# Moving the one-hot transfers to another queue and reordering the opening of a routed-attention + SwiGLU kernel

## The chip, the core and the metric

One core of a Trainium2 chip runs the whole program. The time is device microseconds of one execution, and the kernel before was executed three times. Five engines run their own instruction streams in order: TensorE (PE, matrix products), VectorE (DVE), ScalarE (ACT), GpSimd (POOL) and SyncE (SP, which here only issues transfers). Transfers (DMAs) can be issued from SP, ACT or POOL, each of which issues its own in program order.

## The reference

Attention over 4 batches x 8 heads x 768 tokens x 64, in which a query may only see keys that were assigned to the same one of 16 clusters, followed by a token-wise feed-forward layer on 3072 tokens x 512:

```python
q_assign = np.argmax(np.einsum('bhsd,hcd->bhsc', q_n, c_n), axis=-1)
k_assign = np.argmax(np.einsum('bhsd,hcd->bhsc', k_n, c_n), axis=-1)
mask = q_assign[:, :, :, None] == k_assign[:, :, None, :]
scores = np.where(mask, scale * np.matmul(q, k.transpose(0, 1, 3, 2)), -1e9)
attn = softmax(scores);  x = np.matmul(attn, v)          # heads side by side: 3072 x 512
xn = x / np.sqrt(np.mean(x * x, axis=-1) + 1e-6) * rms_g
out = (silu(xn @ w_gate) * (xn @ w_val)) @ w_out          # 512 -> 1536 -> 512
```

## The kernel before, in words

**The mask as extra rows.** For each head the transposed queries and keys (64 rows, bf16) get 16 more rows that hold the one-hot vector of the token's cluster. One matrix product of 80 rows then gives the score plus a large constant where the clusters agree; the exponential subtracts that constant, so all other pairs vanish. These 80-row operands are the tiles `qext` and `kext`, one per group of four heads, in a ring of four.

**Groups.** Heads are prepared in eight groups of four. For each head PE transposes q and k (`trans`, L192), ACT copies the result out of PSUM (L194) into `qkT`, POOL casts q into `qext` (`qcast`, L198), DVE or ACT casts k into `kext` (`kcast`, L204 and L206), and POOL casts v (`vcast`, L209). `scores_c` multiplies with the centroids (L225), and DVE finds the winner for four heads at once by transpose, maximum, comparison and transpose (L228 to L237), which leaves the one-hot rows in the tile `oh`. `place` then moves them with small transfers into rows 64 to 79 of `qext` and `kext`: per head two for q and two for k, so 16 for a group (L249).

**Units.** The attention runs in eight units (half a batch of queries, all eight heads). For each head there are three score steps (L264, two products into one PSUM tile of the two-tile pool `ps_s`, then an exponential on ACT, L266), and the products with v (`pv`, 18 products of L280 into the single tile `acc`), which are written one head later. After a unit's last head come the root mean square (`rms`: squares on ACT, L299, then a chain of small DVE operations to L312), four transposes (`tx`, L321), the gate and value products (L332) and one unit later the output products (`o`, L355), the copy out of PSUM (`o_sb`, two buffers, L358) and the write to memory (`out_dram`, L360).

**What sets the order.** Each engine's order is the order in which the Python code writes it. In a unit a list `fill` of other work (output products of the unit before last, feed-forward of the last unit, the preparation of a group two units ahead) is spread over the 24 score steps by estimated cost. So at a unit's border the queue of SP holds the group's loads, then that group's 16 one-hot transfers, then the three writes of the output.

**Opening.** Before the first unit the code prepares groups 0 and 1 by hand: eight `warm` products on a constant tile, then group 0 in two pairs of heads (`t0`, `clusters0`, whose two centroid products for q and k share one PSUM tile of `ps_s`), then group 1 by way of the list `first`, then four more `warm` products. Each `warm` product asks for a PSUM tile of its own from a pool with one buffer. The pool of general PSUM tiles, `ps_g`, has three.

Of the kernel before, what the change touches and what calls it, by code (L numbers as in the profile page):

```python
# [9 lines left out]
F32 = mybir.dt.float32  # L10
# [12 lines left out]
def kernel(  # L23
# [12 lines left out]
    nc = tc.nc  # L36
    B, H, S, D = q.shape
# [39 lines left out]
    def load_qk(n, kq=None):  # L77
        if n >= B * H:
            return
        staged[n] = stage.tile([P, 2, ST, D], F32, tag="qk", name="qk")  # L80
        nc.sync.dma_start(out=staged[n][:, 0], in_=src(q, n))
# [18 lines left out]
    nc.vector.memset(warm, 1.0)  # L100

    def busy(n, first=True):
        for i in range(n):
            warm_ps = ps_a.tile([P, 512], F32, tag="acc", name="warm") if first else \
                ps_g.tile([P, 512], F32, tag="gen", name="warm")
            nc.tensor.matmul(warm_ps, lhsT=warm[:, :P], rhs=warm, start=True, stop=True)  # L106

    busy(WARM)

# [86 lines left out]
    def qcast(g, h):  # L196
        for e in range(2):
            nc.gpsimd.tensor_copy(qext[g % 4][:D, h, e * UQ:(e + 1) * UQ], qkT[g, h // 2][e * D:(e + 1) * D, h % 2, 0])  # L198

    def kcast(g, h, early=False):  # L200
        for e in range(2):
            to, of = kext[g % 4][:D, h, e * UQ:(e + 1) * UQ], qkT[g, h // 2][e * D:(e + 1) * D, h % 2, 1]
            if early:
                nc.scalar.activation(to, of, ACT.Copy, scale=1.0 / ZS)  # L204
            else:
                nc.vector.tensor_scalar_mul(to, of, 1.0 / ZS)  # L206

    def vcast(n):
        nc.gpsimd.tensor_copy(vbf[n // HG % 4][:, n % HG, :, :D], stagedv[n])  # L209
# [1 line left out]

    scT = {}

    scps = {}

    def scores_c(g, m, h0=0, h1=HG, early=False):
        if not early:
            ps = ps_g.tile([P, UQ], F32, tag="gen", name="sc")
        else:
            if m == 0:  # L220
                scps[g, h0] = ps_s.tile([P, 2, 512], F32, tag="s", name="sc")
            ps = scps[g, h0][:, m, :UQ]
        r = slice(32 * h0, 32 * h1)
        for h in range(h0, h1):
            nc.tensor.matmul(ps[32 * h:32 * h + 32], lhsT=cblk[:, g * HG % H + h],  # L225
                             rhs=qkT[g, h // 2][:, h % 2, m], start=True, stop=True)
        sct = asg.tile([P, UQ], F32, tag="scT", name="scT", bufs=2)
        nc.vector.transpose(sct[r], ps[r])  # L228
# [8 lines left out]
        nc.vector.transpose(oh[r], ohT[r])  # L237
        ext = (kext if m else qext)[g % 4]
        put.append((g, ext, oh, h0, h1))

    put = []

    def place(q_):

        (g, *_, h0, h1) = put[0]
        for h in range(h0, h1):
            for _, ext, oh, _, _ in put:
                for e in range(2):
                    q_.dma_start(out=ext[D:D + NC, h, e * UQ:(e + 1) * UQ],  # L249
                                 in_=oh[32 * h + e * NC:32 * h + (e + 1) * NC])  # L250
        put.clear()

# [110 lines left out]
    def group_work(g):  # L363
        w = []
        for h in range(HG):
            n = g * HG + h
            w.append((0.25, lambda h=h: trans(g, h, 0)))

            def second(h=h, n=n):
                trans(g, h, 1)  # L370
                qcast(g, h)
                vcast(n)
                if g > 1:
                    kcast(g, h)
                    load_qk(n + NQ)
                    load_v(n + NV)
            w.append((0.25, second))
        w.append((0.7, lambda: scores_c(g, 0)))
        w.append((0.7, lambda: (scores_c(g, 1), place(nc.sync))))
        return w  # L380

    def spread(a, b):
# [30 lines left out]
        for m in range(2):  # L413
            scores_c(0, m, h, h + 2, True)

    first = group_work(1)
# [7 lines left out]
    clusters0(0)  # L424
    t0(2)
    kcast(0, 1, True)
    t0(3)
    kcast(0, 2, True)
    place(nc.gpsimd)
    vcast(0)  # L430
    vcast(1)
    clusters0(2)
    place(nc.sync)
    for _, f in first[:2]:
        f()
    kcast(0, 3, True)
    for _, f in first[2:4]:
        f()
    vcast(2)
    vcast(3)  # L440
    for _, f in first[4:]:
        f()
    for h in range(HG):
        kcast(1, h)
    busy(4)

    def weights():
        for c in range(CC):
# [81 lines left out]
```

## Time and profile before

| | |
|---|---|
| three runs | 397.69, 400.38, 401.13 us (median 400.38) |
| the profiled execution | 400.98 us, of which the span of instructions is 399.1 us |
| PE busy | 357.4 us, 90% of the span |
| ACT busy | 259.5 us, 65% |
| DVE busy | 240.2 us, 60% |
| POOL busy | 60.7 us, 15% |
| granted clock of PE, mean | 0.97 |
| first exponential of unit 0 | 24.30 us after the span's start |
| first exponentials of units 1, 2, 3, 4 | 48.26, 94.45, 143.79, 189.10 us |

How to read it: rows of the timeline give the start in us, the duration, the engine, the line, what is done and how often (x2: two of them, merged), and in brackets how long the engine had stood idle before and what ended that. Rows of the waits give the total, the number and the longest. Rows of a table of windows give the stretch, then for PE, PE's weight load, DVE, ACT and POOL the busy time and the number of instructions, then the granted clock of PE, the share of the transfer engines and the rate.

### The profile page before, as it was taken

The numbers are of one execution on the slowest core, as the hardware profiler recorded it, in microseconds if no ns is written. First come the engines' busy times: TensorE is split into PE (matmuls) and PEld (weight loads), VectorE is DVE, ScalarE is ACT, GpSimd is POOL, SyncE is SP. The second block draws the span as 40 slices with busy tenths as digits, with TensorE's granted clock in tenths as the row PEclk, the third lists the DMA queues.
The fourth block names the chain that finished last, engine by engine and source line by source line (L and its number), as shares of the span: only waits on it lengthen the run. The fifth ranks groups of instructions, "written<-read, shape, count | busy, mean of one in ns | idle before, by whom it ended". The sixth has DMA issues, their size and how long they took to land.

```text
span 399.1 us, 7988 instructions
## 1 busy us (share of the span) xinstructions
PE 357.4 (90%) x3013; PEld 214.4 (54%) x3031; DVE 240.2 (60%) x584; ACT 259.5 (65%) x459; POOL 60.7 (15%) x124
## 2 busy tenths in 40 slices
PE   7778679989779996999979998899979999999896
PEld 3335346564447643665446654566445655664452
DVE  5871156787546775667736675567745646666432
ACT  3768957776638873788548875588746785784230
POOL 2694001441013100320012200121000000000000
PEclk9998969999989999999989999899999999999999
DMA  8719996706232301232022001100020002000102
GB/s 269 220 23 202 207 293 193 214 23 193 72 116 85 119 8 67 87 119 62 15 84 81 2 5 45 51 2 2 14 87 2 1 2 80 2 0 22 60 2 80
DMA packets 24967, 32.03 MB, mean 80 GB/s; under 512 B 4960, under 2 KB 20832, under 8 KB 24928
## 3 DMA queue, kind: packets, MB, share of 16 engines
q1 hardware_dynamic: 21360, 25.91, 20.2%
q0 software_dynamic: 2992, 4.82, 6.7%
q10 hardware_dynamic: 576, 0.79, 0.6%
q8 instruction: 24, 0.39, 0.4%
q14 instruction: 15, 0.12, 0.1%
HBM read 28.35 MB, written 6.29 MB: 87 GB/s over the span
## 4 chain that ended last, share of the span: by engine, by line
PE 59%; SPq 12%; DVE 11%; ACT 9%; DMA 5%; issue 4%; DVEq 0%; ACTq 0%
PE gate L332 15%; PE val L332 14%; SPq L249 11%; PE s L264 10%; PE acc L280 6%; ACT pT L266 5%; PE tq L192 5%; PE o L355 3%; DMA out_dram<-o_sb 3%; PE sc L225 3%; ACT junk L299 2%; PE warm L106 2%; DVE scT L228 2%; DVE oh L237 1%; PE tx L321 1%
## 5 line engine op out<-in xcount | busy, mean ns | idle before, releaser
L266 ACT ACTIVATE pT<-s,off 128x768 bf16<-128x768 f32 x192 | 170.5, 900 | 57.9 <-PE s L264 57.3
L264 PE MATMUL s<-qext,kext 80*128 80x384 bf16 x384 | 96.6, 335 | 5.0 <-ACT pT L266 3.3
L332 PE MATMUL gate<-xnT,wg 128*128 128x384 bf16 x384 | 81.3, 333 | 0.6 <-DVE th L341 0.3
L332 PE MATMUL val<-xnT,wv 128*128 128x384 bf16 x384 | 80.1, 332 | 0.7 <-DVE scT L228 0.7
L341 DVE SCALAR_TENSOR_TENSOR th<-th,gate 128x384 f32<-128x384 f32 x84 | 46.4, 552 | 49.0 <-ACT th L340 48.6
L355 PE MATMUL o<-wo,gvT 128*128 128x512 bf16 x274 | 68.3, 379 | 0.8
L198 POOL CAST qext<-qkT 64x384 bf16<-64x384 f32 x64 | 32.8, 512 | 205.5 <-ACT qkT L194 201.7
L264 PEld LDWEIGHTS <-kext 80*128 80x128 bf16 x384 | 36.8, 100 | 39.3 <-issue 17.6
L280 PE MATMUL acc<-vbf,pT 128*128 128x65 bf16 x1152 | 50.3, 195 | 7.8 <-ACT pT L266 7.1
L280 PEld LDWEIGHTS <-pT 128*128 128x128 bf16 x1152 | 46.3, 99 | 19.2 <-ACT pT L266 9.6
L340 ACT ACTIVATE th<-gate 128x384 f32<-128x384 f32 x84 | 41.0, 488 | 22.9 <-PE gate L332 22.8
L346 DVE SCALAR_TENSOR_TENSOR gvT<-th,val 128x384 bf16<-128x384 f32 x84 | 46.5, 553 | 12.8 <-PE val L332 7.0
L332 PEld LDWEIGHTS <-wg 128*128 128x128 bf16 x384 | 36.8, 99 | 24.2 <-issue 3.5
L332 PEld LDWEIGHTS <-wv 128*128 128x128 bf16 x384 | 36.8, 99 | 23.7 <-issue 2.8
L194 ACT COPY qkT<-tq 128x384 f32<-128x384 f32 x64 | 29.8, 479 | 24.3 <-PE tq L192 23.8
L355 PEld LDWEIGHTS <-gvT 128*128 128x128 bf16 x288 | 26.8, 97 | 27.0
L192 PE MATMUL tq<-ident_f,qk 128*128 128x128 f32 x192 | 32.1, 287 | 1.1 <-ACT qkT L194 0.9
L358 DVE COPY o_sb<-o 128x512 f32<-128x512 f32 x24 | 15.9, 686 | 24.2 <-DMA out_dram<-o_sb 17.5
L192 PEld LDWEIGHTS tq<-ident_f,qk 128*128 128x128 f32 x192 | 24.3, 146 | 8.9 <-ACT qkT L194 1.8
L321 PE MATMUL tx<-ident,xn 128*128 128x128 bf16 x96 | 10.5, 236 | 17.5 <-DVE o_sb L358 16.4
L206 DVE TENSOR_SCALAR kext<-qkT 64x384 bf16<-64x384 f32 x56 | 21.1, 378 | 4.5 <-ACT qkT L194 3.7
L299 ACT ACTIVATE junk<-x 128x384 bf16<-128x384 f32 (+1 forms) x48 | 19.9, 415 | 3.2 <-DVE x L287 2.7
(59 smaller groups left out, 205.6 us busy)
## 6 DMA issues: line engine op xcount, KB each, us to landing
qk<-in_q_dram SPq DMA_DIRECT2D x32, 192.0 KB, 3.4
vs<-in_v_dram SPq DMA_DIRECT2D x32, 192.0 KB, 3.7
out_dram<-o_sb SPq DMA_DIRECT2D x24, 256.0 KB, 2.1
qk<-in_k_dram SPq DMA_DIRECT2D x28, 192.0 KB, 3.7
wg<-in_moe_w_gate_dram POOLq DMA_DIRECT2D x4, 384.0 KB, 9.9
wv<-in_moe_w_val_dram POOLq DMA_DIRECT2D x4, 384.0 KB, 11.3
wo<-in_moe_w_out_dram POOLq DMA_DIRECT2D x3, 512.0 KB, 16.8
qext<-oh SPq DMA_DIRECT2D x60, 12.0 KB, 1.8
```

Source lines behind the costliest of these rows:

```text
L192: nc.tensor.transpose(ps[:, i * P:(i + 1) * P], qk[:, part, 2 * i:2 * i + 2].rearrange("p t d -> p (t d)"), ident_f)
L194: nc.scalar.copy(qkT[g, h // 2][:, h % 2, part], ps)
L198: nc.gpsimd.tensor_copy(qext[g % 4][:D, h, e * UQ:(e + 1) * UQ], qkT[g, h // 2][e * D:(e + 1) * D, h % 2, 0])
L249: q_.dma_start(out=ext[D:D + NC, h, e * UQ:(e + 1) * UQ], in_=oh[32 * h + e * NC:32 * h + (e + 1) * NC])
L264: nc.tensor.matmul(ps[:, j, :UQ], lhsT=kext[g % 4][:KR, hh, kc * P:(kc + 1) * P], rhs=qext[g % 4][:KR, hh, hf * UQ:(hf + 1) * UQ], start=T ...
L266: nc.scalar.activation(pT[u, h][:, 2 * i:2 * i + 2], ps[:, :, :UQ], ACT.Exp, bias=off, scale=scale * ZS)
L280: nc.tensor.matmul(acc[:, h % 2, t], lhsT=pT[u, h][:, kc, t * P:(t + 1) * P], rhs=vbf[g % 4][:, hh, kc % HT * 2 + kc // HT], start=kc == 0 ...
L332: nc.tensor.matmul(ps, lhsT=w[:, c, f * P:(f + 1) * P], rhs=xnT[u][:, c], start=c == 0, stop=c == CC - 1)
L340: nc.scalar.activation(th, ps, ACT.Tanh, scale=0.5)
L341: nc.vector.scalar_tensor_tensor(th, th, 1.0, ps, op0=ALU.add, op1=ALU.mult)
L346: nc.vector.scalar_tensor_tensor(gvT[u][:, f], gates[u], 0.5, ps, op0=ALU.mult, op1=ALU.mult)
L355: nc.tensor.matmul(outs[u], lhsT=gvT[u][:, f, t * P:(t + 1) * P], rhs=wo[:, f], start=f == 0, stop=f == FC - 1)
```

## The change

- `place` takes two queues, one for the q rows and one for the k rows. Groups 0 and 1 issue q's on POOL and k's on SP (before: the first pair of group 0 on POOL, everything else on SP). From group 2 on all 16 are issued on POOL, none on SP.
- In the opening the two centroid products of a pair of heads each get a PSUM tile of their own. ACT's order becomes all eight copies of group 0, then the casts of two heads, four copies of group 1, the other two casts, four copies. v's loads are split: the first four ahead of the first one-hot transfers on SP, the last four behind. The casts of v for group 1 come after its clusters.
- `warm`: five products instead of eight at the start and two instead of four before unit 0, and the products of one call share one PSUM tile.
- In a unit, `pv` of the head before is written after the second score step of a head rather than after the first.

```diff
-    WARM = 8
+    WARM = 5
     def busy(n, first=True):
+        to = ps_a.tile([P, 512], F32, tag="acc", name="warm") if first else \
+            ps_g.tile([P, 512], F32, tag="gen", name="warm")
         for i in range(n):
-            warm_ps = ps_a.tile(...) if first else ps_g.tile(...)
-            nc.tensor.matmul(warm_ps, lhsT=warm[:, :P], rhs=warm, start=True, stop=True)
+            nc.tensor.matmul(to, lhsT=warm[:, :P], rhs=warm, start=True, stop=True)
...
     def scores_c(g, m, h0=0, h1=HG, early=False):
-        if not early:
-            ps = ps_g.tile([P, UQ], F32, tag="gen", name="sc")
-        else:
-            if m == 0:
-                scps[g, h0] = ps_s.tile([P, 2, 512], F32, tag="s", name="sc")
-            ps = scps[g, h0][:, m, :UQ]
+        ps = ps_s.tile([P, UQ], F32, tag="s", name="sc") if early else ps_g.tile([P, UQ], F32, tag="gen", name="sc")
...
-    def place(q_):
+    def place(qq, kq):
         (g, *_, h0, h1) = put[0]
         for h in range(h0, h1):
-            for _, ext, oh, _, _ in put:
+            for (_, ext, oh, _, _), on in zip(put, (qq, kq)):
                 for e in range(2):
-                    q_.dma_start(out=ext[D:D + NC, h, e * UQ:(e + 1) * UQ],
+                    on.dma_start(out=ext[D:D + NC, h, e * UQ:(e + 1) * UQ],
                                  in_=oh[32 * h + e * NC:32 * h + (e + 1) * NC])
...
-        w.append((0.7, lambda: (scores_c(g, 1), place(nc.sync))))
+        w.append((0.7, lambda: (scores_c(g, 1), place(nc.gpsimd, nc.gpsimd if g > 1 else nc.sync))))
...
-    for n in range(H):
+    for n in range(HG):
         load_v(n)
-    nc.sync.dma_start(out=gcol, ...)
-    kcast(0, 0, True)
     clusters0(0)
     t0(2)
-    kcast(0, 1, True)
     t0(3)
-    kcast(0, 2, True)
-    place(nc.gpsimd)
+    place(nc.gpsimd, nc.sync)
+    for n in range(HG, H):
+        load_v(n)
+    nc.sync.dma_start(out=gcol, ...)
+    kcast(0, 0, True)
+    kcast(0, 1, True)
     vcast(0)
     vcast(1)
     clusters0(2)
-    place(nc.sync)
-    (group 1 by its list, kcast(0, 3) and vcast(2), vcast(3) among it, place(nc.sync))
+    (group 1: trans and qcast of heads 0, 1; kcast(0, 2), kcast(0, 3); place(nc.gpsimd, nc.sync);
+     vcast(2), vcast(3); trans and qcast of heads 2, 3; both scores_c; four vcast; place(nc.gpsimd, nc.sync))
     for h in range(HG):
         kcast(1, h)
-    busy(4)
+    busy(2)
...
                 scores(u, h, i)
-                if i == 0 and (u, h) != (0, 0):
+                if i == 1 and (u, h) != (0, 0):
                     pv(u, h - 1) if h else pv(u - 1, H - 1)
```

**SP's queue at the border of units 2 and 3**, here the last two one-hot transfers of a group (`oh`), the three output writes (`o_sb`) and the next loads, before:

```order
L249 DMA qext0_146<-oh_2136 16x384 x2
L249 DMA kext0_150<-oh_2175 16x384 x2
L360 DMA out_0_dram<-o_sb_2272 128x512
L360 DMA out_0_dram<-o_sb_2317 128x512
L360 DMA out_0_dram<-o_sb_2367 128x512
L81 DMA qk_2430<-in_q_dram 128x384
```

and the same place of SP's queue after the change:

```order
L81 DMA qk_2056<-in_q_dram 128x384
L82 DMA qk_2056<-in_k_dram 128x384
L88 DMA vs_2059<-in_v_dram 128x384
L353 DMA out_0_dram<-o_sb_2259 128x512
L353 DMA out_0_dram<-o_sb_2284 128x512
L353 DMA out_0_dram<-o_sb_2333 128x512
```

The 16 one-hot transfers that stood between the group's last load and the first write are gone from SP.

**POOL's queue in unit 1**, where groups 2 and 3 are prepared one after the other, after the change (the last casts of group 2, `qext2` and `vbf2`, its 16 one-hot transfers, of which the last four are shown as two rows, and the first casts of group 3):

```order
L242 DMA qext2_138<-oh_1199 16x384 x2
L242 DMA kext2_142<-oh_1235 16x384 x2
L198 CAST qext3_139<-qkT_1265 64x384 x2
L209 CAST vbf3_147<-vs_783 128x6x64
L198 CAST qext3_139<-qkT_1265 64x384 x2
```

Before the change the casts of group 3 followed the casts of group 2 directly on POOL.

**ACT's order in the opening**, before (L194 copies out of PSUM, L204 casts k, L266 is the first exponential):

```order
L194 COPY qkT<-tq 128x384 x4
L204 ACTIVATE kext_150<-qkT 64x384 x2
L194 COPY qkT<-tq 128x384 x2
L204 ACTIVATE kext_150<-qkT 64x384 x2
L194 COPY qkT<-tq 128x384 x2
```

and after:

```order
L194 COPY qkT<-tq 128x384 x8
L204 ACTIVATE kext_140<-qkT 64x384 x4
L194 COPY qkT<-tq 128x384 x4
L204 ACTIVATE kext_140<-qkT 64x384 x4
L194 COPY qkT<-tq 128x384 x4
L259 ACTIVATE pT<-s,off 128x768 x22
```

The casts moved behind the copies of the second pair of heads; their number is the same.

More of the change, by code (lines that the diff above doesn't have):

```diff
@@ L102, in busy @@
     def busy(n, first=True):
+        to = ps_a.tile([P, 512], F32, tag="acc", name="warm") if first else \
+            ps_g.tile([P, 512], F32, tag="gen", name="warm")
         for i in range(n):
-            warm_ps = ps_a.tile([P, 512], F32, tag="acc", name="warm") if first else \
-                ps_g.tile([P, 512], F32, tag="gen", name="warm")
-            nc.tensor.matmul(warm_ps, lhsT=warm[:, :P], rhs=warm, start=True, stop=True)
+            nc.tensor.matmul(to, lhsT=warm[:, :P], rhs=warm, start=True, stop=True)
     busy(WARM)
@@ L212 @@
     scT = {}
-    scps = {}
     def scores_c(g, m, h0=0, h1=HG, early=False):
-        if not early:
-            ps = ps_g.tile([P, UQ], F32, tag="gen", name="sc")
-        else:
-            if m == 0:
-                scps[g, h0] = ps_s.tile([P, 2, 512], F32, tag="s", name="sc")
-            ps = scps[g, h0][:, m, :UQ]
+        ps = ps_s.tile([P, UQ], F32, tag="s", name="sc") if early else ps_g.tile([P, UQ], F32, tag="gen", name="sc")
         r = slice(32 * h0, 32 * h1)
@@ L371, in second @@
                 qcast(g, h)
+                kcast(g, h)
                 vcast(n)
[L373 to L376, printed above, removed]
+                load_qk(n + NQ)
+                load_v(n + NV)
             w.append((0.25, second))
         w.append((0.7, lambda: scores_c(g, 0)))
-        w.append((0.7, lambda: (scores_c(g, 1), place(nc.sync))))
+        w.append((0.7, lambda: (scores_c(g, 1), place(nc.gpsimd, nc.gpsimd if g > 1 else nc.sync))))
         return w
@@ L414, in clusters0 @@
             scores_c(0, m, h, h + 2, True)
-    first = group_work(1)
     t0(0)
@@ L419 @@
     t0(1)
-    for n in range(H):
+    for n in range(HG):
+        load_v(n)
+    clusters0(0)
+    t0(2)
+    t0(3)
+    place(nc.gpsimd, nc.sync)
+    for n in range(HG, H):
         load_v(n)
@@ L423 @@
     kcast(0, 0, True)
-    clusters0(0)
-    t0(2)
     kcast(0, 1, True)
-    t0(3)
-    kcast(0, 2, True)
-    place(nc.gpsimd)
     vcast(0)
@@ L432 @@
     clusters0(2)
-    place(nc.sync)
-    for _, f in first[:2]:
-        f()
+    for h in range(2):
+        trans(1, h, 0)
+        trans(1, h, 1)
+        qcast(1, h)
+    kcast(0, 2, True)
     kcast(0, 3, True)
-    for _, f in first[2:4]:
-        f()
+    place(nc.gpsimd, nc.sync)
     vcast(2)
     vcast(3)
-    for _, f in first[4:]:
-        f()
+    for h in range(2, HG):
+        trans(1, h, 0)
+        trans(1, h, 1)
+        qcast(1, h)
+    for m in range(2):
+        scores_c(1, m)
+    for n in range(HG, H):
+        vcast(n)
+    place(nc.gpsimd, nc.sync)
     for h in range(HG):
         kcast(1, h)
-    busy(4)
+    busy(2)
     def weights():
```

## The prediction

> **What bounds the kernel now.** I read the page's busy shares first, then the waits in total, then the timeline at the borders of the units, then PE's clock there, and the opening last.
>
> ```profile
> PE 357.4 (90%) x3013; PEld 214.4 (54%) x3031; DVE 240.2 (60%) x584; ACT 259.5 (65%) x459; POOL 60.7 (15%) x124
> PE tx L321 <- DVE o_sb L358: 16.4, 6, 4.0
> ```
>
> PE is busy nine tenths of the span, so time is won where PE stands idle or runs slowly. Its largest wait is six stalls before `tx`, 16.4 us together, in which it waits for DVE's copy of the output. One of them in full, at the border of units 2 and 3:
>
> ```profile
> 152.12 1.28 DVE L358 COPY o_sb<-o 128x512 f32<-128x512 f32 x2
> 154.59 1.02 PE L355 MATMUL o<-wo,gvT 128*128 128x512 bf16 x4
> 155.19 1.22 SPq L249 DMA_DIRECT2D kext<-oh  x2
> 156.52 3.32 SPq L360 DMA_DIRECT2D out_dram<-o_sb  x3
> 158.79 0.69 DVE L358 COPY o_sb<-o 128x512 f32<-128x512 f32 x1 [3.21 <-DMA out_dram<-o_sb]
> 159.53 0.33 PE L321 MATMUL tx<-ident,xn 128*128 128x128 bf16 x3 [3.25 <-DVE o_sb L358]
> ```
>
> There are two `o_sb` buffers and three copies. The first copy ends at 152.12 + 1.28/2 = 152.8, but its write is issued at 156.52, since SP is still issuing one-hot transfers (to 155.19 + 1.22 = 156.41). The third copy waits for that write to land, and PE waits for the third copy. Unit 7's border, which has no one-hot transfers ahead of its writes, shows what is left then:
>
> ```profile
> 367.17 1.28 DVE L358 COPY o_sb<-o 128x512 f32<-128x512 f32 x2
> 370.01 0.69 DVE L358 COPY o_sb<-o 128x512 f32<-128x512 f32 x1 [1.56 <-DMA out_dram<-o_sb]
> 370.76 0.65 PE L321 MATMUL tx<-ident,xn 128*128 128x128 bf16 x6 [1.46 <-DVE o_sb L358]
> ```
>
> From the start of the first copy to the third it takes 370.01 - 367.17 = 2.84 us when SP is free.
>
> The stalls cost a second time. Windows right behind them:
>
> ```profile
> 157.92:161.34 3.42, 1.81 (x14) 1.21 (x14) 2.08 (x5) 0.48 (x1) 0.30 (x1) 1.00 0.49 187
> 161.34:164.75 3.41, 3.41 (x39) 2.39 (x38) 1.82 (x4) 3.05 (x5) 1.22 (x3) 1.00 0.28 75
> 202.30:205.71 3.41, 1.34 (x12) 0.97 (x12) 1.92 (x5) 0.60 (x2) 0.00 (x0) 1.00 0.56 215
> 205.71:209.12 3.41, 3.41 (x13) 1.94 (x12) 1.27 (x3) 1.56 (x4) 1.52 (x3) 0.50 0.04 16
> 113.55:116.96 3.41, 3.41 (x15) 1.75 (x13) 1.07 (x3) 1.87 (x3) 1.52 (x3) 0.50 0.19 74
> 250.08:253.50 3.42, 2.74 (x14) 1.88 (x14) 2.03 (x5) 0.48 (x1) 0.81 (x2) 0.50 0.20 78
> 297.87:301.28 3.41, 3.41 (x28) 2.10 (x27) 1.00 (x2) 1.39 (x2) 0.00 (x0) 0.50 0.00 0
> ```
>
> Behind four of the five stalls that have one-hot transfers in front, PE's granted clock is 0.50 for 3.41 us; a stretch with 1.34 us of PE work was followed by the half clock, one with 1.81 was not.
>
> **The borders, units 2 to 6.** The other four of the five stalls:
>
> ```profile
> 112.72 0.33 PE L321 MATMUL tx<-ident,xn 128*128 128x128 bf16 x3 [4.00 <-DVE o_sb L358]
> 204.37 0.33 PE L321 MATMUL tx<-ident,xn 128*128 128x128 bf16 x3 [2.78 <-DVE o_sb L358]
> 250.76 0.48 PE L321 MATMUL tx<-ident,xn 128*128 128x128 bf16 x3 [2.75 <-DVE o_sb L358]
> 296.32 0.65 PE L321 MATMUL tx<-ident,xn 128*128 128x128 bf16 x6 [2.19 <-DVE o_sb L358]
> ```
>
> With SP free, the third copy at 158.79 could start at 152.12 + 2.84 = 154.96, but its product ends at 154.59 + 1.02 = 155.61: it would come 3.1 us sooner, and PE would wait some 0.2 us in place of 3.25. What is late next is thus the third product itself, PE's own work. The five stalls are 4.00 + 3.25 + 2.78 + 2.75 + 2.19 = 14.97; less about 0.3 each I take **-13.5 us** (bounds -14.9 and, if unit 7's 1.46 us stays at each, -7.7).
>
> The half clock: from 159.53 to 204.37 are 44.84 us without it, from 204.37 to 250.76 are 46.39 with it and a like stall, so one costs 1.55. Four of them: **-6.2 us** (bounds -6.2 and 0). [...]
>
> **The 96 one-hot transfers of groups 2 to 7, now on POOL.**
>
> ```profile
> L249 POOL DMA_DIRECT2D qext<-oh x4 | 2.1, 531 | 0.0
> 28.45 0.65 POOL L178 DMA_DIRECT2D wv<-in_moe_w_val_dram  x1
> 26.52 3.65 DVE L206 TENSOR_SCALAR kext<-qkT 64x384 bf16<-64x384 f32 x8
> 161.04 1.07 POOL L198 CAST qext<-qkT 64x384 bf16<-64x384 f32 x2 [25.98 <-ACT qkT L194]
> 82.45 0.58 DVE L237 STREAM_TRANSPOSE oh<-ohT 128x384 bf16<-128x384 bf16 x1
> 82.85 0.51 POOL L209 CAST vbf<-vs 128x384 bf16<-128x384 f32 x1
> 123.10 0.90 ACT L266 ACTIVATE pT<-s,off 128x768 bf16<-128x768 f32 x1
> ```
>
> POOL takes 0.53 us for one, so 16 take 8.5. In units 2 to 5 POOL stands idle 25.98 us there: nothing. In unit 1 they stand in front of group 3's casts: group 2's k rows are ready at 82.45 + 0.58 = 83.03, 14 transfers later (the first two, q's, are out) it is 90.4, four heads' casts (1.07 + 0.51 each) end at 96.8, four transfers of group 3 at about 99 and landed near 101 (2 us is an estimate below the 3.3 that 192 KB took to land in the opening), and they must be there for unit 2's fifth head, whose exponential is at 123.10 now and would be near 115. **0 us**, with 14 us of cover. SP's loads of v wait for those casts, but SP itself was held by the same 16 transfers until now.
>
> **The opening, to the first exponential.**
>
> ```profile
> 6.55 1.29 PE tq L192 x6
> 1.18 0.42 SPq L81 DMA_DIRECT2D qk<-in_q_dram  x1
> qk<-in_q_dram SPq DMA_DIRECT2D x1, 192.0 KB, 3.3
> 7.79 0.93 PE L192 MATMUL tq<-ident_f,qk 128*128 128x128 f32 x4
> PE sc L225 <- DVE scT L228: 1.4, 2, 0.7
> 22.70 0.39 PE warm L106
> 24.30 2.49 ACT pT L266 x3
> ```
>
> Eight `warm` products hold PE until 6.55, though head 0's q landed at 1.18 + 3.3 = 4.5. Five without a wait between them end before that. Head 1's data came by about 6.3 (the next transfers landed near there), so its transposes move from 7.79 to some 6.4: -1.4. The separate tiles take out the two waits of 0.7 for DVE, both on PE's path: -1.4, of which I count 0.9, as ACT's copies and casts then press. Two `warm` products fewer, and no wait between the others, before the first scores: four at 0.39 become two at about half that, -0.7 or more. Against it: the first six transposes took 1.29 us, and a gap of PE before them may keep it slow longer. ACT's casts behind the copies are the same casts; 0. Sum **-3.0 us** (bounds -4 and -1). Weights stay behind POOL's opening work, near 28 us as now, and are needed far later; 0.
>
> **`pv` behind the second score step.**
>
> ```profile
> L266 ACT ACTIVATE pT<-s,off 128x768 bf16<-128x768 f32 x25 | 21.1, 899 | 5.6 <-PE s L264 5.6
> 26.84 0.60 PE acc L280 x14
> 27.44 0.34 PE s L264 x2
> PE acc L280 <- ACT pT L266: 7.1, 12, 1.9
> ```
>
> In unit 0 ACT sets the pace. The group's row, taken from 24.3 to 48.3, shows 5.6 us of waiting for scores, 3.1 of it (the longest single wait) before the first exponential, so 2.5 between. The pattern is in the chain: PE does 0.60 of `acc` after an exponential ends, then the scores of 0.34, together longer than the exponential of 2.49/3 = 0.83 that runs meanwhile. With the scores first they are ready after 0.34. I take **-2.0 us** (bounds -2.5 and -0.5). In the other units PE sets the pace, and its waits for `pT` are 7.1 us in all; but the score step that now comes first needs the tile which the same exponential frees, and the squares start later: -0.5 (bounds -2.5 and +1).
>
> **Sum.** -13.5 - 6.2 + 0 - 3.0 - 2.0 - 0.5 = -25.2. The profiled execution took 400.98 us, 1.9 more than its span; the median of the runs is 400.38, so it stands for it. 400.98 - 25.2 = **375.8, so 376 us**.
>
> **The rivals.**
> *The half clock stays.* The dips could have a cause other than the stalls, or come at other places, as happens once in unit 0 without any such stall. [...] Against it: all four lie right behind a stall, none elsewhere from 60 us on. 376 + 6.2 = 382 us. Chance 0.13.
> *The write itself takes SP's place.* The wait of unit 7 stays at each of the five borders: 7.7 in place of 13.5, so 382 us. Against it: at the other borders the third product ends later than the 2.84 us. Chance 0.08.
> *Slower: POOL's queue becomes the bound in unit 1.* If one transfer took t on POOL, group 3 would be ready for unit 2's fifth head at 83.0 + 14t + 6.3 + 4t + 2, and the next three heads each 4t later against 5.3 us of a head's work. Up to t = 1.3 nothing is lost (115). From t = 2.2 the loss, 18t - 24 + 3(4t - 5.3), eats the 25 us, and beyond it the kernel is slower; at six times the row's 0.53, 3.2 us, it is 33 + 22 = 55, so 431 us. [...] Against it: at 28.45 a weight transfer was issued on POOL in 0.65 amid eight of DVE's casts of k. Chance 0.04. [...]
> *Little comes of it.* The borders' gain is given back by a wait that I don't see, and it stays within 1%: 0.04.
> *Better.* All bounds at their lower ends and one dip fewer in unit 0: 370 us or less. Chance 0.07.
>
> **Numbers.** The forecast has the remaining 0.64, with a range of its own of 372 to 380. 370 to 383 takes in the two rivals at 382 and leaves out the better, the small and the slower ones, 0.15. A difference of 1% is about what can be told from no change here. Faster 0.92, same 0.04, slower 0.04.
>
> **What would show it.** SP issues the first write within 0.2 us of the first copy's end; the waits of PE for `o_sb` fall to about 3 us (unit 7 and rests); the granted clock is 1.00 behind the borders; third copies lie some 42 us apart. The first exponential starts near 21.3, unit 1's near 43. POOL's row for L242 shows about 0.53 us. I am wrong if POOL's transfers take more than 1.3 us, if the clock falls at other places, or if PE waits for the third copy all the same.

## The result, and the profile after

The kernel after takes 377.6 us (median of four runs, 375.2 to 380.43) where the kernel before, on the same chip, takes 400.75 us: 0.9439 of the time, with a 95% interval of 0.9349 to 0.9528. The forecast was 376 us. The profiled execution took 375.2 us with a span of 373.4 us. Four more runs of the same program on another chip (the experiment after_again) gave 375.7 to 379.76 us; the median of all eight is 379.06 us, and where an experiment below is set against the kernel after, this number is meant. Beside each experiment the kernel before was run again, and the ratios leave out runs of more than 1.5% above the fastest of the same kernel, so they can differ by a few tenths of a per cent from the quotient of the medians. Of the experiments one run is left out below: in it PE's clock was 0.75 nearly throughout, and it took 456.02 us.

The busy shares on the page of the kernel after, and from its waits the two that concern `o_sb`:

```profile
PE 347.5 (93%) x3008; PEld 210.3 (56%) x3026; DVE 239.8 (64%) x584; ACT 258.2 (69%) x459; POOL 111.3 (30%) x228
```

```profile
DVE o_sb L351 <- DMA out_dram<-o_sb: 7.7, 5, 1.6
PE tx L314 <- DVE o_sb L351: 3.1, 5, 1.5
```

PE waits 3.1 us for `o_sb` where it waited 16.4. DVE still waits five times for a write to land, 7.7 us in all, but little of that reaches PE. The border of units 2 and 3 in the timeline of the kernel after, to be held against the same border before:

```profile
142.18 1.03 PE L348 MATMUL o<-wo,gvT 128*128 128x512 bf16 x4
142.22 1.27 DVE L351 COPY o_sb<-o 128x512 f32<-128x512 f32 x2
142.92 3.16 SPq L353 DMA_DIRECT2D out_dram<-o_sb  x3
143.37 1.03 PE L348 MATMUL o<-wo,gvT 128*128 128x512 bf16 x4
145.03 0.69 DVE L351 COPY o_sb<-o 128x512 f32<-128x512 f32 x1 [1.54 <-DMA out_dram<-o_sb]
145.78 0.33 PE L314 MATMUL tx<-ident,xn 128*128 128x128 bf16 x3 [0.17 <-DVE o_sb L351]
```

The first copy ends at 142.22 + 1.27/2 = 142.86 and its write is issued at 142.92. The third copy starts 2.81 us after the first (2.84 at unit 7's border before), and PE waits 0.17 us for it in place of 3.25. What the third copy waits for is still the landing of the first write: its product had ended at 143.37 + 1.03 = 144.40.

The first and the last of the five borders of units 2 to 6:

```profile
102.99 0.69 DVE L351 COPY o_sb<-o 128x512 f32<-128x512 f32 x1 [1.57 <-DMA out_dram<-o_sb]
271.19 0.69 DVE L351 COPY o_sb<-o 128x512 f32<-128x512 f32 x1 [1.52 <-DMA out_dram<-o_sb]
```

They lie (271.19 - 102.99)/4 = 42.05 us apart. Before, by the `tx` rows behind the third copies, it was (296.32 - 112.72)/4 = 45.90.

PE's clock is 1.00 behind all of them. The only half clock ahead of the program's last microseconds lies at the border of units 0 and 1, in these windows (length, then busy time of PE, PEld, DVE, ACT and POOL, then the granted clock):

```profile
40.89:44.30 3.41, 1.84 (x25) 1.12 (x24) 0.38 (x2) 3.41 (x8) 0.00 (x0) 1.00 1.08 214
44.30:47.71 3.41, 2.08 (x11) 0.82 (x10) 1.74 (x10) 3.25 (x9) 0.00 (x0) 0.50 1.07 211
47.71:51.13 3.42, 2.68 (x28) 1.81 (x26) 2.45 (x9) 1.09 (x2) 0.00 (x0) 0.50 1.13 218
```

It lasts to 54.54. Before, such a stretch lay there too, and the windows are told of further down, since much of the rest of the time turned out to hang on them.

The one-hot transfers on POOL, as groups:

```profile
L242 POOL DMA_DIRECT2D qext<-oh x64 | 31.4, 495 | 33.6 <-DVE oh L230 33.4 <-issue 0.3
L242 POOL DMA_DIRECT2D kext<-oh x48 | 23.5, 495 | 11.9 <-DVE oh L230 10.7 <-DVE inv L278 1.3
```

One takes 495 ns, 112 of them, where 531 ns was forecast.

The opening in the timelines of PE and ACT, and the first exponential of unit 1:

```profile
6.51 0.48 PE L167 MATMUL c_ps<-ident_f,c_n 128*128 128x128 f32 x1 [0.54 <-DVE c_n L161]
6.78 1.49 PE L192 MATMUL tq<-ident_f,qk 128*128 128x128 f32 x6
18.82 0.55 PE L192 MATMUL tq<-ident_f,qk 128*128 128x128 f32 x3 [1.96 <-ACT qkT L194]
21.95 3.27 ACT L259 ACTIVATE pT<-s,off 128x768 bf16<-128x768 f32 x4 [2.06 <-PE s L257]
43.15 1.70 ACT L259 ACTIVATE pT<-s,off 128x768 bf16<-128x768 f32 x2
```

The first exponential comes at 21.95 us (24.30 before; 21.3 forecast) and unit 1's first at 43.15 (48.26 before; 43 forecast). Head 1's transposes start at 6.78, not at 6.4: between the two heads PE transposes the centroids, and those wait for DVE. At 18.82 PE has waited 1.96 us for one of ACT's copies.

### The profile page after: what moved, and what is told of

The parts are those of the page before. It is cut to its first block, busy times and chain, and to the rows that moved or that the text cites. A ratio compares the mean times of both kernels' runs of the same rounds, so it can differ in the third digit from the quotient of the medians.

```text
span 373.4 us, 7988 instructions
## 1 busy us (share of the span) xinstructions
PE 347.5 (93%) x3008; PEld 210.3 (56%) x3026; DVE 239.8 (64%) x584; ACT 258.2 (69%) x459; POOL 111.3 (30%) x228
## 4 chain that ended last, share of the span: by engine, by line
PE 67%; DVE 12%; ACT 11%; DMA 4%; issue 3%; POOL 3%; DVEq 0%; ACTq 0%
PE gate L325 16%; PE val L325 16%; PE s L257 12%; PE o L348 8%; PE acc L273 6%; ACT pT L259 5%; PE tq L192 4%; PE sc L218 3%; DMA out_dram<-o_sb 3%; ACT junk L292 3%; DVE o_sb L351 2%; DVE xn L305 2%; ACT qkT L194 2%; DMA vs<-in_v_dram 1%; PE tx L314 1%
## 5 line engine op out<-in xcount | busy, mean ns | idle before, releaser
L259 ACT ACTIVATE pT<-s,off 128x768 bf16<-128x768 f32 x192 | 169.6, 901 | 43.5 <-PE s L257 43.1
L257 PE MATMUL s<-qext,kext 80*128 80x384 bf16 x384 | 95.4, 330 | 7.2 <-ACT pT L259 6.6
L325 PE MATMUL gate<-xnT,wg 128*128 128x384 bf16 x384 | 79.2, 327 | 2.6 <-ACT qkT L194 1.8
L325 PE MATMUL val<-xnT,wv 128*128 128x384 bf16 x384 | 78.6, 327 | 0.6 <-DVE scT L221 0.6
L273 PEld LDWEIGHTS <-pT 128*128 128x128 bf16 x1152 | 44.0, 98 | 9.5 <-ACT pT L259 0.6
L273 PE MATMUL acc<-vbf,pT 128*128 128x65 bf16 x1152 | 46.1, 194 | 0.5 <-ACT pT L259 0.5
L242 POOL DMA_DIRECT2D qext<-oh x64 | 31.4, 495 | 33.6 <-DVE oh L230 33.4
L194 ACT COPY qkT<-tq 128x384 f32<-128x384 f32 x64 | 29.6, 479 | 12.4 <-PE tq L192 12.1
L242 POOL DMA_DIRECT2D kext<-oh x48 | 23.5, 495 | 11.9 <-DVE oh L230 10.7
## 6 DMA issues: line engine op xcount, KB each, us to landing
wo<-in_moe_w_out_dram POOLq DMA_DIRECT2D x3, 512.0 KB, 21.3
```

Source lines behind the costliest of these rows:

```text
L194: nc.scalar.copy(qkT[g, h // 2][:, h % 2, part], ps)
L242: on.dma_start(out=ext[D:D + NC, h, e * UQ:(e + 1) * UQ], in_=oh[32 * h + e * NC:32 * h + (e + 1) * NC])
L257: nc.tensor.matmul(ps[:, j, :UQ], lhsT=kext[g % 4][:KR, hh, kc * P:(kc + 1) * P], rhs=qext[g % 4][:KR, hh, hf * UQ:(hf + 1) * UQ], start=T ...
L259: nc.scalar.activation(pT[u, h][:, 2 * i:2 * i + 2], ps[:, :, :UQ], ACT.Exp, bias=off, scale=scale * ZS)
L273: nc.tensor.matmul(acc[:, h % 2, t], lhsT=pT[u, h][:, kc, t * P:(t + 1) * P], rhs=vbf[g % 4][:, hh, kc % HT * 2 + kc // HT], start=kc == 0 ...
L325: nc.tensor.matmul(ps, lhsT=w[:, c, f * P:(f + 1) * P], rhs=xnT[u][:, c], start=c == 0, stop=c == CC - 1)
```

## The experiments

**The queue alone, and the queue undone.** In the first, the kernel before gets only this:

```diff
-        w.append((0.7, lambda: (scores_c(g, 1), place(nc.sync))))
+        w.append((0.7, lambda: (scores_c(g, 1), place(nc.gpsimd if g > 1 else nc.sync))))
```

> The kernel before with one edit: from group 2 on the 16 one-hot transfers are issued on POOL. My theory: the five waits of PE for the output copy shrink from 15.0 us to about 1.5 and the half clock behind them goes, so about 13.5 + 6.2 = 19.7 us less, near 381 us. Rival, the opening and the later products with v carry the gain: at most 5 us less, 395 us or more. Rival, the half clock has another cause: 13.5 us less, near 387, with four stretches at 0.50 after 60 us.

Measured: 382.75 us beside 400.74, 0.957 (0.9489 to 0.9651). PE's wait for `o_sb` among the waits of this kernel:

```profile
PE tx L321 <- DVE o_sb L358: 1.5, 1, 1.5
```

Of the 16.4 us of stalls 1.5 is left, unit 7's. At the border of units 2 and 3 the copies and the third product are these:

```profile
146.96 1.27 DVE L358 COPY o_sb<-o 128x512 f32<-128x512 f32 x2
149.39 1.02 PE L355 MATMUL o<-wo,gvT 128*128 128x512 bf16 x4
150.45 0.69 DVE L358 COPY o_sb<-o 128x512 f32<-128x512 f32 x1
```

Here, with `pv` in its old place, the third copy starts right behind its product (149.39 + 1.02 = 150.41), and no write keeps it waiting. So 18.0 us by the medians, 17.2 by the ratio, of the first pair's 23 come from the queue, and the prediction's terms for it are 13.5 + 6.2 = 19.7.

In the second, the kernel after gets only the reverse:

```diff
-        ... place(nc.gpsimd, nc.gpsimd if g > 1 else nc.sync)
+        ... place(nc.sync, nc.sync)
```

> The kernel after, but the one-hot transfers of groups 2 to 7 are back on SP. My theory: the five stalls come back, about 19 us more than after, near 396 us, third copies 45 to 47 us apart in place of 42. Rival, the parts overlap and the other edits alone already hide the writes: within 5 us of after.

Measured: 399.59 us beside 400.74, 0.9962 (0.9924 to 1.0). PE's waits for `o_sb` are back at 16.8 us, and the queue is worth 20 us here. The other parts without it are worth 1.2 us, not the 5.5 of the prediction; the larger part of the reason stands in these windows of the profile:

```profile
15.26:18.67 3.41, 1.45 (x16) 0.79 (x18) 2.98 (x6) 3.19 (x8) 3.28 (x7) 1.00 0.41 128
18.67:22.08 3.41, 3.08 (x17) 0.93 (x10) 2.75 (x6) 0.01 (x1) 3.32 (x7) 0.51 0.61 144
22.08:25.50 3.42, 2.26 (x27) 1.18 (x26) 3.32 (x6) 3.42 (x5) 3.27 (x7) 0.99 0.04 11
25.50:28.91 3.41, 3.15 (x30) 1.80 (x27) 2.08 (x6) 3.16 (x4) 3.41 (x8) 0.51 0.13 29
```

Up to here this program is the kernel after, and yet it has the half clock at 18.67 and for three windows from 25.50 on, where that kernel's first profile has none. Its first exponential came at 22.07 us, and unit 1's at 46.32: unit 0 took 24.2 us in place of 21.2.

**The writes on POOL's queue, the one-hot transfers left on SP.** In the kernel before:

```diff
-            nc.sync.dma_start(out=rows[:, 2 * t + hf], in_=o)
+            nc.gpsimd.dma_start(out=rows[:, 2 * t + hf], in_=o)
```

> The kernel before, with the one-hot transfers left on SP and only the 24 output writes moved to POOL's queue. My theory (the loss is the write's place behind the one-hot transfers and nothing else of the queue): the same gain as from moving the one-hot transfers, 18 to 20 us, near 381. Rival (what helps is that SP's loads or the one-hot rows come sooner): no gain, 400.

Measured: 385.16 us, 0.9609 (0.955 to 0.9667). Its border of units 2 and 3:

```profile
146.18 1.22 SPq L249 DMA_DIRECT2D kext<-oh  x2
146.66 1.28 DVE L358 COPY o_sb<-o 128x512 f32<-128x512 f32 x2
147.65 1.14 POOL L360 DMA_DIRECT2D out_dram<-o_sb  x2 [18.05 <-DVE o_sb L358]
148.95 1.20 SPq L249 DMA_DIRECT2D kext<-oh  x2
150.42 0.69 DVE L358 COPY o_sb<-o 128x512 f32<-128x512 f32 x1 [0.30 <-PE tx L321]
```

The one-hot transfers run on SP during and after the copies, as before; only the write has another queue, and the third copy no longer waits for it. What cost the time was the order in one queue, not that many small transfers were under way. The time is 2.4 us more than in the queue-alone kernel, 4.5 us between the two profiles, and that comes late: unit 7's first exponential is only 0.4 us later (303.33 and 302.94 us), one window at 352.4 us has the half clock, the last output copy is at 377.5 us in place of 374.99, and the remaining 2 us lie behind it.

**The stalls kept, but filled.** In the kernel before, 40 small dummy products into unused columns of `acc` behind the second of the border's transposes, in units 2 to 6:

```diff
+        if 0 < u < NU - 2:
+            w[1:2] = [w[1], (0.0, lambda: filler(u + 1, 40))]
```

> The kernel before with 40 dummy products of 122 columns (about 2 us of PE work, results unused) put in front of the third transpose of units 2 to 6, where PE stalls. The write still comes late. My theory (the stall of PE is what drops the clock): the granted clock stays 1.00 behind the borders, about 6 us less, near 394, with third copies 44 to 45 us apart at all borders. [...]

Measured: 396.65 us, 0.992 (0.9878 to 0.9962). The third copies come as late as before (DVE waits 16.9 us in all for writes to land). Windows at the borders of units 2 and 4:

```profile
110.45:113.86 3.41, 1.12 (x16) 0.94 (x14) 1.34 (x3) 0.00 (x0) 0.00 (x0) 0.99 0.41 157
113.86:117.28 3.42, 3.38 (x17) 2.00 (x15) 1.33 (x4) 1.70 (x3) 1.51 (x3) 0.51 0.22 81
199.20:202.61 3.41, 3.41 (x56) 2.81 (x53) 0.75 (x2) 1.61 (x2) 0.00 (x0) 1.00 0.37 132
202.61:206.02 3.41, 2.63 (x27) 1.92 (x25) 2.08 (x5) 0.71 (x2) 1.00 (x2) 1.00 0.29 112
```

With PE kept busy through the stall the half clock is gone at three of the four borders; at the first, where the dummies ran out and PE waited another 2.3 us, so that the window held 1.12 us of work, it stayed. The time is 4.1 us less by the medians, 3.2 by the ratio. Between the two profiles the three units behind these borders are shorter by 1.50, 0.66 and 1.56 us from first exponential to first exponential, so a dip is worth some 1.2 us, where the prediction took 1.55 from one pair of borders. Another 1.1 us lies in unit 3, where neither profile has a dip; there the third copy came 5.47 us after the first in place of 6.67, so not all of the 4.1 us is the clock's. The rest of the queue's gain is the stalls themselves.

**POOL's queue made longer.** The slower rival said that POOL's queue would bind in unit 1. In the kernel after, each one-hot transfer from group 2 on is followed by one (three) smaller ones, 16 x 256 (16 x 84), into a tile that nobody reads any more; each holds POOL for 489 (488) ns:

```diff
+                    for i in range(1 if g > 1 else 0):      # 3 in the second kernel
+                        on.dma_start(out=warm[...], in_=oh[...])
```

> The kernel after, with one more transfer of the same kind, into a tile that nobody reads any more, behind each of the 96 one-hot transfers on POOL. A place takes POOL about 1.0 us in place of 0.5. The prediction gave 14 us of cover in unit 1 and no loss up to 1.3 us a place: 0 us, so within 1 us of the kernel after (378). Rival, that POOL's queue is already near the bound: each of the 18 places that the prediction counts adds 0.5 us, 8 us or more, so 386 us.

> The kernel after, with three more such transfers behind each of the 96 on POOL, so about 2.0 us a place. By the prediction's formula for its slower case the loss is 18 x 2.0 - 24 + 3 x (8.0 - 5.3) = 20 us, all of it ahead of unit 2's last heads: about 397 us. If there is more cover than the prediction saw (group 3's casts not waited for as early as it says), less: 378 to 388.

Measured: 382.74 us (382.44 to 383.97) with two, 396.47 us (394.69 to 399.67) with four transfers a place; 3.7 and 17.4 us more than the kernel after. The second agrees with the prediction's formula, which gave 20, but not by its mechanism. The timeline of SP, DVE and PE at unit 2's border in the kernel with four, and SP's largest wait for POOL:

```profile
118.07 0.33 SPq L88 DMA_DIRECT2D vs<-in_v_dram  x1
118.49 5.52 SPq L357 DMA_DIRECT2D out_dram<-o_sb  x3
...
122.96 0.69 DVE L355 COPY o_sb<-o 128x512 f32<-128x512 f32 x1 [17.47 <-DMA out_dram<-o_sb]
...
123.70 0.48 PE L318 MATMUL tx<-ident,xn 128*128 128x128 bf16 x3 [16.96 <-DVE o_sb L355]
```

```profile
SPq L88 <- POOL vbf L209: 78.6, 14, 30.3
```

No head of group 3 is waited for. SP's load of v waits for POOL's cast of the v before it, that cast stands behind the one-hot transfers on POOL, and the output's write stands behind the load on SP: the same write as before the change, held by another row of its queue. PE's stall of 16.96 us, against 1.06 there in the kernel after, is 15.9 of the 17.4 us. How much room the kernel after has at this place, on SP:

```profile
92.34 0.33 SPq L88 DMA_DIRECT2D vs<-in_v_dram  x1
100.85 3.19 SPq L353 DMA_DIRECT2D out_dram<-o_sb  x3
```

From 92.67 to 100.85 SP is free: that is 8.2 us of cover (the time by which POOL may fall behind before a write is late), not 14. With two transfers a place that is used up nearly to the end (the load at 101.85, the write at 104.43); there the write needed 3.36 us from its issue to the third copy, 1.2 more than in the kernel after, while POOL issued transfers from 101.81 to 105.88, and two windows at half clock follow at 107.8 us. What made that write slower, no run shows.

**pv undone, and the opening undone.** The kernel after with `if i == 0` for `pv`:

> The kernel after with pv put back behind the first score step; the rest as after. The prediction's term for this part was 2.0 us in unit 0 and 0.5 elsewhere: by it the first exponential of unit 1 comes 2.0 us later than in the kernel after, measured from the first of unit 0 (21.2 us there), and the time is 2.5 us longer, about 380.5 beside 378. Rival: in unit 0 ACT's own work sets the pace and the order gives nothing: within 0.5 us in the profile, and no difference in the times.

Measured: 381.05 us (379.52 to 381.81), 0.9542 (0.9489 to 0.9594) of the kernel before. Its first exponentials of units 0 and 1 on ACT:

```profile
22.70 1.69 ACT L259 ACTIVATE pT<-s,off 128x768 bf16<-128x768 f32 x2 [2.06 <-PE s L257]
45.71 1.69 ACT L259 ACTIVATE pT<-s,off 128x768 bf16<-128x768 f32 x2
```

Unit 0 takes 23.01 us at full clock, where it took 21.20 in the first profile of the kernel after: 1.8 us for the order of `pv`, in the profile, and 2.0 us in the times. Units 3 to 6, which have no dip in either profile, take 42.18, 42.17, 42.17 and 38.10 us from first exponential to first exponential, and 42.04, 42.06, 42.06 and 37.93 in the kernel after: 0.5 us together.

The kernel of the queue alone with `if i == 1`, so the kernel after with the opening of before:

> The kernel before with the one-hot transfers of groups 2 to 7 on POOL and pv behind the second score step; only the opening is that of before. The prediction's term for the opening was 3.0 us; the profiles showed 2.35 at the first exponential. So the first exponential near 24.3 us (21.95 in the kernel after), and 2.4 to 3 us longer, about 380.5 to 381. Rival: the earlier start is given back, since the weights' and the loads' transfers or ACT set what comes behind: unit 2's first exponential at the same time as in the kernel after, and no difference.

Measured: 379.87 us (377.67 to 383.52), 0.9514 (0.9455 to 0.9572). This is 0.8 us more than the kernel after, and cannot be told from no difference. Its first exponential comes at 24.25 us. The queue-alone kernel differs from this one in `pv` alone, and from the one before it in the opening alone: its 382.75 us against 379.87 and 381.05 make 2.9 us for `pv` and 1.7 us for the opening. All four differences point the same way, but they are between runs on different occasions and the intervals of the two ratios overlap in each pair, so none of them, the 2.0 us included, is clear of the noise alone.

**The kernel after once more.**

> The kernel after, unchanged, once more on the chip of the others. By the theory of windows its runs lie between 375 and 381 us, those with more windows at half clock being the longer ones, and each half-clock stretch in its profile begins a multiple of 3.41 us behind another. By the rival (a slow chip, or a cause in memory) the spread has nothing to do with the clock.

Measured: 379.12 us (375.7 to 379.76), 0.953 (0.947 to 0.9589). Windows of its profile:

```profile
9.74:13.16 3.42, 3.42 (x14) 1.88 (x11) 2.70 (x5) 0.60 (x2) 0.30 (x2) 1.00 0.97 322
13.16:16.57 3.41, 3.41 (x23) 1.89 (x21) 3.23 (x6) 3.37 (x8) 3.27 (x7) 1.00 0.31 110
23.40:26.81 3.41, 2.13 (x22) 1.05 (x21) 3.27 (x6) 3.25 (x5) 3.22 (x7) 1.00 0.02 5
26.81:30.22 3.41, 3.06 (x30) 1.83 (x27) 3.31 (x9) 2.99 (x5) 3.41 (x7) 0.50 0.10 24
```

The same program has 10.2 us at half clock in unit 0 this time, from 26.81 on, and unit 0 takes 24.24 us (first exponentials at 23.56 and 47.80). The first full clock on record begins at 13.16 us (10.17 in the first profile; the windows' view shows 1.00 ahead of that record, but PE, busy all the time in both rows, gets through 14 products before it and 23 after), and the first exponential is 1.6 us later. The eight runs fall in two groups: 375.2 to 376.14 us with mean clocks of 0.984 to 0.986, and 379.05 to 380.43 with 0.967 to 0.977.

**The clock kept by dummies.** In the kernel after, dummy products of 0.2 us each in a row ((1.03 - 0.38)/3 = 0.22: four products of this size, 128x512, take 1.03 us in the kernel after, one alone 0.38) where PE waits early: five before the last transposes of the opening, and 2, 3, 1, 5 and 2 around the border of units 0 and 1:

```diff
+        if h == 3:
+            busy(5)
...
+                extra = {(0, 7, 2): 2, (1, 0, 0): 3, (1, 0, 1): 1, (1, 1, 0): 5, (1, 1, 1): 2}.get((u, h, i), 0)
+                if extra:
+                    busy(extra, False)
```

> The kernel after, with dummy products (0.2 us each) where PE waits early: five before the last transposes of the opening (PE waits 1.96 us there for a copy), 2, 3, 1, 5 and 2 around the border of units 0 and 1 (waits of 0.5 to 1.2 us). Nothing is left out. Theory: the granted clock is decided for windows of 3.41 us, and the window behind one with under some 1.6 to 2.2 us of PE work runs at half; the windows lie otherwise in every run, and so the runs of the kernel after differ by 4 to 5 us (375.2 to 380.4). With these places filled, the half clock from 44.3 to 54.5 us goes, the mean clock is 0.99 or more in every run, and the time is 372 to 374 us with a spread below 2 us. Rival: the clock falls by another rule, or the dummies stand in the way of the exponentials as much as the clock gives: within 1 us of the kernel after, with the same spread.

Measured: 373.49, 376.67, 379.03, 380.42 and 380.92 us, and the run at 0.75 that is left out. The best run is 1.7 us below any of the kernel after, but the spread did not shrink. Once more, for a profile:

> The kernel after with the dummy products around the opening and the border of units 0 and 1, once more, for a profile of an ordinary run. Its runs so far were 373.5, 376.7, 379.0, 380.4 and 380.9, with mean clocks of 0.998 to 0.981, and one of 456.0 in which the clock was 0.75 nearly throughout. By the theory of windows the profile shows no half clock before 60 us in a run with 0.995 or more, and in the others windows at half clock behind places that the dummies do not cover. By a rival, that the dummies bring the clock down themselves, the profile shows a clock of 0.75 or 0.5 behind stretches in which PE was busy all the time.

Measured: 378.39 us (377.09 to 379.56), 0.9476 (0.9414 to 0.9537). The half clock at 44 to 54 us is gone, and 26.4 to 36.7 us has it, as in the kernel after's second profile: the place not covered was the beginning of unit 0. So one or two dummies more behind eight of unit 0's first ten score steps:

```diff
+                extra = {(0, 0, 0): 2, (0, 0, 1): 2, (0, 0, 2): 2, (0, 1, 0): 2, (0, 1, 2): 1, (0, 2, 0): 1,
+                         (0, 2, 2): 1, (0, 3, 0): 1, (0, 7, 2): 2, (1, 0, 0): 3, ...
```

> The kernel with the dummy products of c1, and one or two more behind eight of the first ten score steps of unit 0, where four of five profiles of the kernel's order show half clock for 10.2 us (26 to 37 us) and unit 0 3.0 us longer for it (24.2 in place of 21.2 us from its first exponential to unit 1's). Theory: the window ahead of that stretch holds some 2.1 to 2.25 us of PE work; with 12 dummies of 0.2 us it holds 3 us, the half clock does not come in any run, unit 0 takes 21.2 us every time, and the runs lie at 372 to 375 us. Rival: the dummies stand ahead of scores that ACT waits for; unit 0 then takes 22 to 23.5 us in every run, and the time is that of the kernel after, 376 to 379.

Measured: 375.29 us (373.4 to 376.44, six runs) beside 399.23, 0.9401 (0.9349 to 0.9452). The windows at the start of unit 0:

```profile
21.48:24.89 3.41, 3.41 (x21) 1.50 (x17) 3.24 (x7) 2.09 (x3) 3.28 (x7) 1.00 0.40 92
24.89:28.31 3.42, 3.11 (x41) 1.99 (x40) 3.33 (x7) 3.42 (x5) 3.31 (x7) 1.00 0.04 11
```

PE has over 3 us of work in each, and the half clock does not follow. One window at the border of units 0 and 1 still has it, behind one with 2.06 us of work:

```profile
48.79:52.20 3.41, 2.06 (x17) 1.12 (x17) 2.87 (x10) 1.24 (x2) 0.00 (x0) 1.00 1.12 217
52.20:55.62 3.42, 3.42 (x12) 1.60 (x11) 1.32 (x4) 1.47 (x3) 0.00 (x0) 0.50 1.15 262
```

Unit 0 takes 21.15 us (first exponentials at 22.80 and 43.95), the mean clock is 0.994 or more in all six runs, and the spread is 3.0 us where it was 5.2. The dummies cost ACT nothing that can be seen: it waits 42.9 us for scores in the profile, and 43.1 in the first of the kernel after. This version, 3.8 us below the kernel after by the medians, is the fastest of the study, by runs on different occasions, each beside the kernel before: the interval of its ratio lies below that of the kernel after's second set (0.947 to 0.9589) and inside that of the first (0.9349 to 0.9528).

## Why the prediction was right

**The borders** (-13.5): right in size. The five stalls of 14.97 us have become 3.1 - 1.47 = 1.6, where 1.5 was left over in the forecast. What is late next is, as said, the product itself, but only as long as `pv` keeps its place (the queue alone, and `pv` undone, where PE waits for `o_sb` at unit 7 alone). In the kernel after the third product ends 2.18 us after the first copy's start, 3.49 before, so the landing of the write is late instead. That is the rival of the write in SP's place, in kind, but at a smaller price: PE waits 1.06 us at the first border and 0.2 or less at the others, where the rival had 1.46 at each. The queue-alone and the writes-on-POOL kernels tell the cause from its neighbours: it is enough to part the write from the one-hot transfers.

**The half clock** (-6.2): the cause was right, and the size a little high. All four dips went with the stalls; kept busy in the stall, PE kept its clock at three borders of four, and a dip was worth some 1.2 us, so four some 5. The queue alone gave 17.2 to 18.0 of the 19.7 us of both terms. The rival that these dips have another cause falls.

**The one-hot transfers on POOL** (0): the time was right, 495 ns for 531, and so was the 0. The cover was not. The prediction read it for the consumer of the one-hot rows, 14 us and nothing lost up to 1.3 us a transfer. The first that becomes late is the output's write, by way of POOL's cast of v and SP's load of v, with 8.2 us of cover; at 2.0 us a place it cost nearly all of the 17.4 us. At 1.0 us a place that write was not held yet, and still 3.7 us were lost, where the forecast had none: the write landed later and the clock fell behind it. The prediction names that wait of SP and dismisses it, since SP was held by the transfers until then; who stands behind it in the queue was not followed. The slower rival reckons with six times the row's 0.53 us, 3.2 us a transfer; no run shows that: the longest of the 112 in the kernel after held POOL for 0.69 us, with DVE busy for 0.64 of it.

**The opening** (-3.0): too large. The first profiles differ by 2.35 us at the first exponential. Over five profiles with the old opening it lies at 24.25 to 24.64 (mean 24.37), over six with the new one at 21.95 to 23.56 (mean 22.55): 1.8 us. In the times it is 0.8 and 1.7 us in the two pairs, neither to be told from zero. Two steps failed: the centroids' transposes between head 0 and head 1 were overlooked (0.54 us for DVE), and the remark that PE may stay slow longer without its early products was priced at nothing. The second shows in two profiles whose windows lie alike, the kernel before and then the one with `pv` undone, which has the new opening:

```profile
4.33:7.74 3.41, 3.24 (x11) 1.69 (x9) 1.88 (x11) 0.48 (x1) 0.00 (x0) 1.00 1.04 366
4.18:7.60 3.42, 2.15 (x8) 1.52 (x9) 2.79 (x14) 0.96 (x2) 1.02 (x2) 1.00 0.97 345
```

Behind the first the full clock is on record from 7.74 us; behind the second only from 11.01, a window later. In the new opening it begins anywhere from 4.86 to 13.16 us (7.02 to 8.53 in the old). Between the two profiles of the kernel after, where it begins 2.99 us apart, the first exponential moves by 1.6 us. Part of that may be the load: head 1's q, taken to be there by 6.3, landed at 5.91 us in the first of them and at 7.18 in the second, and with `pv` undone at 7.30, with PE waiting 0.43 us for it. How much each is worth stays open.

**pv** (-2.0 in unit 0, -0.5 elsewhere): 2.0 and 2.9 us in the two pairs of times, so the sum fits as far as the noise lets it be seen. The 1.8 us in unit 0 are what the full clock gives, and the 0.5 us of the other units is there in units 3 to 6. Five of six profiles with this order (the kernel after twice, the queue undone, the two with more on POOL, the opening undone) have the half clock there and take 24.2 to 24.4 us, no better than the 23.0 to 24.0 of the five with the old order. Both orders have a thin window there, of 2.13 to 2.25 us of PE work with the new and 1.96 to 2.39 with the old; but with the scores first the half clock, where it comes behind that, lasts three windows, as PE has 3.06 to 3.18 us to do in the first two, and one window with the old order (3.11 to 3.19 us). So the mechanism is right, but what it gives in unit 0 depends on where the windows lie, and that is luck.

The sum of -25.2 stands beside -23.15 by the first medians and -21.7 by that of all eight runs (379.06 and 400.75); by the second set's own ratio, 0.953, it is only some -19 us. So the total was too high by 2 to 6 us, and that 376 came so near to 377.6 is in part the luck of the first four runs, two of which lie in the faster group. The part that was left out is the run-to-run place of the half clock, worth some 4 us, which lies in the range but has no term in the sum. A clock that falls at other places was named as a sign of being wrong, and in unit 0 and behind it, it does so; at the borders, which the term was for, it does not.

## What to carry to other kernels

In an in-order queue ask not only what an operation feeds but what stands behind it: the write was held by 16 small issues before (at the border of units 2 and 3 it was issued at 156.52 us, its copy had ended at 152.8), and would next be held by a load that waits for a cast (PE's stall of 16.96 us with four transfers a place). A gain that comes from a better order was worth less here where PE had too little to do to keep its clock: unit 0 took 24.24 us with the half clock and 21.20 without. So count PE's work for every 3.413 us, the window seen here, at any phase, and fill what is thin with products that nobody reads: of the 76 windows with up to 2.26 us of it 37 were followed by the half clock, of the other 1,220 none. Where runs of one program differ by a per cent (375.2 to 380.43 us here), look at the clock in two profiles before explaining it by the program.

## What the runs showed of the hardware

The granted clock went by windows of 3.413 us. In every profile the half-clock stretches start a whole number of them apart: in the kernel before at 113.55, 205.71, 250.08 and 297.87 us, so 27, 13 and 14 windows. Where they lie relative to the program differs from run to run: the kernel after has 10.2 us at half clock from 44.30 us on in its first profile and from 26.81 us on in its second, 5.12 windows apart.

If the 13 profiles (the kernel before, the kernel after and the experiments but the one at 0.75) are cut at these places, and the time in which PE has a product running is added up for each window, there are 1,296 windows at full clock between the first record of it and 366 us. All 19 with less than 1.58 us were followed by the half clock, 18 of the 57 from 1.58 to 2.26 us, and none of the other 1,220. Back to full took more work than staying there: at half clock, windows with even 3.06 us of 3.41 of PE work were followed by another at half (ten of eleven with 3.06 or 3.07), and all from 3.19 on by the full clock. The border is not clean: one window with 2.74 us (the kernel before, at 250.08 us) was followed by the full clock, and so were six of the eight between 3.07 and 3.19. It fits that the dip in unit 0 lasts three windows: in the second profile of the kernel after PE has 3.06, 3.07 and 3.19 us of work in them, at half clock, and the full clock follows.

One run of an experiment (c1_clock_kept) had a clock of 0.75 from 10.4 us to its end, but for 10.2 us at half clock, and the 0.75 began ahead of the first product that the experiment added (18.1 us). No run shows what brought it.
